# A routed MoE kernel: ReLU's output transposed by VectorE and DRAM in place of TensorE, the second product two slots behind, weight splits placed in branches of each slot

## The chip, the cores and the metric

The kernel runs on one core of a Trainium2 chip. The time is that of one execution on the device, in microseconds (us); lower is better. A core has five engines with instruction streams of their own: TensorE (PE), VectorE (DVE), ScalarE (ACT), GpSimd (POOL) and SyncE (SP). They meet only at semaphores and through transfers (DMA) that an engine issues and the DMA engines carry out.

## The reference

A block-causal attention over 8 batches, 8 heads, 576 positions and a head width of 64 gives 4608 rows (tokens) of 512 numbers. Each row is then sent to one of 8 experts:

```python
logits = x @ w_gate
expert_idx = np.argmax(logits, axis=1)
probs = np.exp(logits - logits.max(-1, keepdims=True))
probs /= probs.sum(-1, keepdims=True) + 1e-09
gate_w = probs[np.arange(N), expert_idx]
for e in range(E):                       # 8 experts
    mask = expert_idx == e
    if not mask.any():
        continue
    xe = x[mask]
    h = np.maximum(xe @ w1[e], 0.0)      # 512 -> 1024
    ye = h @ w2[e]                       # 1024 -> 512
    out[mask] = gate_w[mask, None] * ye
```

Everything is float32. Which expert a row goes to is known only when the attention has been computed. For the inputs that are timed, the experts get 896, 0, 1030, 58, 512, 192, 384 and 1536 rows.

## The kernel before, in words

Two parts follow each other: the attention with the router (until about 377 us), which the change leaves as it is, and the class `Experts`, where all of the change lies.

**Slots.** The rows of an expert are taken in slots of 128; an expert with n rows has n/128 slots, rounded up. Here that is 7, 9, 1, 4, 2, 3 and 12 slots for the seven experts that have rows, one after the other: slots 0-6, 7-15, 16, 17-20, 21-22, 23-25 and 26-37. The first 36 slots exist whatever the data; for 36 and 37 every engine branches (`tail`, L1173). A small table that DVE works out (`slots`, L732 to L748) tells each slot's expert.

**One slot.** A slot t has these steps; `period(t)` writes them into the engines' streams:

- `gather`: POOL fetches the slot's 128 rows from the DRAM copy `xd` by an indirect DMA.
- `rows_in`: PE transposes the rows, four 128x128 pieces into the PSUM tile `px` (L853).
- `rows_act`, `rows_pool`: ACT rounds `px` to `xh` (L863) and copies it to `xf` (L866); POOL takes `xl = xf - xh` (L872). A float32 number is so split into a high and a low part, and a product is made of three: high by high, low by high, high by low.
- `first_pe`: the first product, 48 matmuls 128x128 by 128x512, 24 each into the PSUM tiles `ph` and `o` (L894). Its weights w1 are split in the same way.
- `relu_act`: ACT writes ReLU of `ph` and `o` to `h` (L930), 128 rows by 512 each.
- `hidden_pe`, `hidden_act`, `hidden_low`: PE transposes each half of `h` into `pt` (L938, four matmuls), ACT rounds it to the high part (L948; the trace calls this tile `low`, after the pool that it lies in) and copies it to `hf` (L952), and POOL subtracts (L958).
- `second_pe`: the second product, 24 matmuls into `py` (L978), in two halves of 12.
- `out_act`, `out_pool`: ACT scales `py` by the gate to `y` (L995), POOL scatters it to the output by an indirect DMA (L1001).

**Order.** It is written out by hand. On PE a period is: first product of t, `rows_in` of t+1, transposes of the first half of h of t, half of the second product of t-1, transposes of the second half, the other half of the second product of t-1. So the second product runs one slot behind the first.

**Weights.** An expert's weights are eight chunks of 128x1024: four of w1, four of w2. SP loads them (L1095) into five buffers `raw`; DVE copies each chunk to its high part (L1102) and subtracts for the low part (L1108). There are two halves of the weight buffer `w`, used in turn by the experts. DVE splits the next expert's w1 as soon as the first product of the last slot of the expert before the running one is done, and its w2 as soon as that slot's second product is done (a wait on a count read from the table, L1157). This is a loop over the eight experts ahead of all of the slots: it has no place in the slots' order.

**End.** `finish` does the last slot's second product and the last two slots' outputs.

The PE order, the ACT order and the lines above are the ones that the change touches.

## Time and profile before

| | |
|---|---|
| median of 3 runs | 861.5 us (858.24 to 861.5) |
| the profiled execution, its own time | 861.02 us |
| the profiled execution, its span | 859.2 us |
| mean granted TensorE clock in it | 0.994 |
| attention and router | to about 377.6 us |
| start of the expert part, until the slots run evenly | 377.6 to 405.3 us |
| slots 3 to 37, 35 slots | 405.3 to 840.1 us |
| the last output | 840.1 to 859.2 us |

The span runs from the first instruction of the trace to its last; what is left to the execution's own time, 1.8 us, lies around it. In the rows of a profile, a line such as L938 is a line of the kernel before, an engine's name stands ahead of the operation, and `out<-in` are the tiles that it writes and reads. `PEclk` is the clock that TensorE was granted, 1.00 being full speed.

### The profile page before, as it was taken

The numbers are of one execution on the slowest core, as the hardware profiler recorded it, in microseconds if no ns is written. First come the engines' busy times: TensorE is split into PE (matmuls) and PEld (weight loads), VectorE is DVE, ScalarE is ACT, GpSimd is POOL, SyncE is SP. The second block draws the span as 40 slices with busy tenths as digits, with TensorE's granted clock in tenths as the row PEclk, the third lists the DMA queues.
The fourth block names the chain that finished last, engine by engine and source line by source line (L and its number), as shares of the span: only waits on it lengthen the run. The fifth ranks groups of instructions, "written<-read, shape, count | busy, mean of one in ns | idle before, by whom it ended". The sixth has DMA issues, their size and how long they took to land.

```text
span 859.2 us, 15869 instructions
## 1 busy us (share of the span) xinstructions
PE 828.8 (96%) x4936; PEld 634.4 (74%) x4936; DVE 391.3 (46%) x1144; ACT 457.0 (53%) x1154; POOL 394.9 (46%) x394
## 2 busy tenths in 40 slices
PE   4999999999999999989999999999999999999993
PEld 2666666666666676668888888888888888888882
DVE  3567676767676767668615000058356450000000
ACT  3777677777777777724443443343344434433430
POOL 4121244444444624255746444556566564445451
PEclk9999999999999999999999999999999999999997
DMA  5229726363635355425614311146436431111110
GB/s 174 73 96 188 206 96 164 96 161 111 157 103 139 120 119 179 102 48 194 219 50 138 133 50 50 38 135 209 166 123 245 142 111 38 50 50 37 38 51 28
DMA packets 45687, 99.33 MB, mean 116 GB/s; under 512 B 7585, under 2 KB 10913, under 8 KB 45602
## 3 DMA queue, kind: packets, MB, share of 16 engines
q1 hardware_dynamic: 38082, 78.26, 31.3%
q0 software_dynamic: 7520, 19.97, 6.8%
q8 instruction: 49, 0.80, 0.4%
q14 instruction: 36, 0.29, 0.1%
HBM read 76.76 MB, written 21.98 MB: 115 GB/s over the span
## 4 chain that ended last, share of the span: by engine, by line
PE 91%; DMA 3%; ACT 1%; POOL 1%; issue 1%; SPq 1%; DVE 0%; POOLq 0%; ACTq 0%; DVEq 0%
PE py L978 24%; PE ph L894 12%; PE o L894 12%; PE o L270 11%; PE ya L169 6%; PE xa L169 4%; PE pt L938 4%; PE o L305 3%; PE px L853 2%; DMA xd<-xg 2%; ACT pb L200 1%; PE o L299 1%; DMA qd<-qT 1%; PE o L158 1%; DMA out<-y,idx 1%
## 5 line engine op out<-in xcount | busy, mean ns | idle before, releaser
L978 PE MATMUL py<-w,low 128*128 (+1 forms) x912 | 231.5, 403 | 0.1
L978 PEld LDWEIGHTS py<-w,low 128*128 128x128 f32 x912 | 166.4, 189 | 35.4 <-issue 0.5
L112 POOL TENSOR_SCALAR q<-qd 128x640 f32<-128x640 f32 x32 | 58.0, 1812 | 189.4 <-PE o L158 124.3
L1102 DVE CAST w<-raw 128x1024 fp32r<-128x1024 f32 x60 | 52.9, 931 | 185.6 <-PE o L894 135.1
L958 POOL TENSOR_TENSOR low<-hf,low 128x512 fp32r<-128x512 f32 x72 | 98.9, 1374 | 35.6 <-ACT hf L952 35.6
L872 POOL TENSOR_TENSOR xl<-xf,xh 128x512 fp32r<-128x512 f32 x38 | 51.4, 1354 | 90.8 <-ACT xf L866 90.6
L1108 DVE TENSOR_TENSOR w<-raw,w 128x1024 fp32r<-128x1024 f32 x60 | 82.6, 1434 | 0.0
L948 ACT CAST low<-pt 128x512 fp32r<-128x512 f32 x76 | 45.7, 601 | 58.2 <-PE pt L938 56.9
L200 ACT ACTIVATE pb<-ya,neg 128x320 f32<-128x320 f32 (+2 forms) x96 | 50.1, 525 | 48.1 <-DVE neg L185 48.1
L894 PE MATMUL o<-w,xh 128*128 x280 | 75.6, 392 | 0.0
L894 PE MATMUL ph<-w,xh 128*128 x280 | 75.6, 392 | 0.0
L1001 POOL DMA_INDIRECT out<-y,idx x35 | 40.0, 1144 | 65.9 <-ACT y L995 65.9
L169 PE MATMUL ya<-kd,q 64*128 64x192 f32 (+2 forms) x192 | 61.8, 456 | 2.7 <-ACT pb L200 2.7
L930 ACT ACTIVATE h<-o 128x512 f32<-128x512 f32 x37 | 22.2, 599 | 74.7 <-PE o L894 74.7
L169 PE MATMUL yb<-kd,q 64*128 64x192 f32 (+2 forms) x192 | 61.8, 457 | 0.0
L995 ACT ACTIVATE y<-py,xg 128x512 f32<-128x512 f32 x38 | 26.2, 690 | 66.3 <-PE py L978 60.8
L894 PEld LDWEIGHTS ph<-w,xh 128*128 128x128 f32 x280 | 52.6, 188 | 11.6
L894 PEld LDWEIGHTS o<-w,xh 128*128 128x128 f32 x280 | 52.6, 188 | 11.5
L930 ACT ACTIVATE h<-ph 128x512 f32<-128x512 f32 x37 | 22.2, 599 | 73.1 <-PE ph L894 73.1
L689 POOL DMA_INDIRECT tab<-toks,posi x40 | 41.8, 1044 | 27.3 <-DVE run L656 13.8
L200 ACT ACTIVATE pb<-yb,neg 128x192 f32<-128x192 f32 (+2 forms) x96 | 49.8, 526 | 0.4 <-DVE neg L185 0.4
L952 ACT COPY hf<-pt 128x512 f32<-128x512 f32 x76 | 46.3, 609 | 6.0 <-POOL low L958 5.2
(953 smaller groups left out, 1805.3 us busy)
## 6 DMA issues: line engine op xcount, KB each, us to landing
raw<-w SPq DMA_DIRECT2D x60, 512.0 KB, 5.5
qd<-qT SPq DMA_DIRECT2D x32, 352.0 KB, 3.4
v<-vt SPq DMA_DIRECT2D x32, 352.0 KB, 4.6
kd<-kT SPq DMA_DIRECT2D x32, 288.0 KB, 4.0
xd<-xt SPq DMA_DIRECT2D x7, 1026.0 KB, 8.5
xd<-xg SPq DMA_DIRECT2D x9, 256.5 KB, 12.1
xg<-w SPq DMA_DIRECT2D x8, 256.0 KB, 3.9
xd<-x SPq DMA_DIRECT2D x8, 128.0 KB, 3.8
```

The costliest lines, as they stand in the source:

```text
L112: self.nc.gpsimd.tensor_scalar(q, self.raws[m][0][:, 0 : 512 + P], 0.125, None, ALU.mult)
L169: ins = mm(out, q[r, 128 * (i - 1) : 128 * i], k[r, o : o + n], start=True, stop=True, skip_group_check=True)
L200: ins = self.nc.scalar.activation(dst, src, AF.Exp, bias=self.neg[m][:, c : c + 1], scale=1.0, accum_out=self.sums[m][:, c : c + 1])
L270: self.nc.tensor.matmul(out[r], self.raws[m][2][:, slot], self.ph[m, bank][:, c0:c1], start=t in (0, 5), stop=t in (4, 5), skip_group_chec ...
L872: pool.tensor_sub(self.xl, self.xf, self.xh).then_inc(sem["xp"], 1)
L894: m = pe.matmul(self.ph[f], x[:, P * k : P * k + P], weights(k, f, part), start=start and k == 0, stop=stop and k == 3,)
L948: act.copy(self.hh[t % 2][:, f], self.pt[f]).then_inc(sem["ha"], 1)
L952: act.copy(self.hf, self.pt[f]).then_inc(sem["ha"], 1)
L958: engine.tensor_sub(self.hl[t % 2][:, f], self.hf, self.hh[t % 2][:, f]).then_inc(sem["hp"], 1)
L978: m = pe.matmul(self.py[t % 2], h[:, c // 4, P * (c % 4) : P * (c % 4) + P], wf[:, bass.ds(off + (base + 512 * c), 512)], start=n == 0, st ...
L1102: dve.tensor_copy(hi, raw[m % nr]).then_inc(sem["wh"], 1)
L1108: dve.tensor_sub(lo, raw[m % nr], hi).then_inc(sem["wd"], 1)
```

## The change

**The transposes of h.** After the change PE does not transpose h from slot 3 on, and ACT and POOL do not read it out of PSUM. `blocks(t, f)`: DVE transposes each half of h in blocks of 32x32 into `hblk`, laid out so that a block stands where it is needed within its 32 partitions. `leave(t)`: ACT issues one DMA of `hblk` (128x1024, 512 KB) to a DRAM buffer `there`. `enter(t)`, a slot later: ACT issues four DMAs of 128 KB back from DRAM, each for 32 partitions, which brings the blocks into the right partitions. `split_act`: one ACT copy of 128x1024 makes the high part; `split_pool`: two POOL subtractions of 128x512 the low part. They stand in place of four ACT instructions and two of POOL.

**The lag.** The second product of a slot runs two slots behind its first product: period t has `second_pe(t - 2)`. At the transition, period 3 still has the second product of slot 2, period 4 has none, and period 5 has that of slot 3. The output is three slots behind. Five buffers `xg` instead of four hold the gathered rows, and ACT issues DMAs, which it did not do in the slots before.

**The weight splits.** The loop over the experts is gone. Eight chunks are four units of two chunks (two copies, two subtractions). DVE's stream has, in each period t after `blocks(t)`, the w2 units of period t-1 and the w1 units of period t; which of them are done is read from a table `pk` in each slot and decided by branches. `pieces`, 18 small DVE operations with one copy more in `slots`, makes that table. The plan it gives: the next expert's units 0 to 3 go one to each of the running expert's first slots, and where it has fewer than four slots, several to the first: an expert with three slots has units 0 and 1 in its first slot, with two slots 0 to 2, with one slot all four. For slots 0 and 1 the plan counts as if the first expert began at slot 2. The raw buffers are four instead of five, and SP loads only the experts that have rows (48 loads in place of 56 in that loop).

On PE, between the last matmul of the first product and the first of the second, the stream of one slot reads before:

```order
L894 MATMUL o<-w,xh 128x512
L853 MATMUL px<-ident,xg_192 128x128 x4
L938 MATMUL pt_4960<-ident,h_4955 128x128 x4
L966 REGISTER_ALU
L978 ISA
L978 MATMUL py_4962<-w,low_75 128x512
```

and after:

```order
L940 MATMUL o<-w,xh 128x512
L899 MATMUL px<-ident,xg_193 128x128 x4
L1066 UNCONDITIONAL_BRANCH
L1066 REGISTER_ALU
L1083 ISA
L1083 MATMUL py_4969<-w,low_77 128x512
```

The four transposes of h (`pt`) are gone, the same holds for the four in the middle of the second product, and a jump has come in that closes the block of DVE's branches.

ACT's stream of one slot, with the semaphores that an instruction waits for in brackets, reads before (y is scaled, h is ReLU's output, `low` the high part of the transposed h, `hf` its copy):

```order
L995 ACTIVATE y<-py_4962,xg_192 128x512 [waits y,mm2]
L930 ACTIVATE h_4955<-ph_4958 128x512 [waits ht,mm1]
L930 ACTIVATE h_4956<-o 128x512 [waits ht,mm1]
L863 CAST xh<-px 128x512 [waits mm1,xt]
L866 COPY xf<-px 128x512 [waits xp]
L948 CAST low_75<-pt_4960 128x512 [waits mm2,ht]
L952 COPY hf<-pt_4960 128x512 [waits hp]
L948 CAST low_75<-pt_4961 128x512 [waits mm2,ht]
L952 COPY hf<-pt_4961 128x512 [waits hp]
```

and after:

```order
L1100 ACTIVATE y<-py_4969,xg_192 128x512 [waits y,mm2]
L1033 DMA high<-there_59 32x4x256 [waits ln,hn,dw]
L1033 DMA high<-there_59 32x4x256 x3
L978 ACTIVATE h_4962<-ph_4965 128x512 [waits tb,mm1]
L978 ACTIVATE h_4963<-o 128x512 [waits tb,mm1]
L909 CAST xh<-px 128x512 [waits mm1,xt]
L912 COPY xf<-px 128x512 [waits xp]
L1022 DMA there_60<-hblk 128x1024 [waits tb]
L1044 CAST low_77<-high 128x1024 [waits mm2,dr]
L1066 UNCONDITIONAL_BRANCH
```

Two transfers of a slot now stand in ACT's stream with waits in front: the read of slot t-1 ahead of ReLU of slot t, waiting for the write of slot t-1 (`dw`); and the rounding of slot t-1 behind it, waiting for that read (`dr`).

DVE's stream before has nothing of the slots, only the splits. The start of one expert's w1, with the read of the count (`si`) of the slots ahead of the running expert, is:

```order
L1157 TENSOR_LOAD si
L1157 ISA x2
L1160 ISA
L1102 CAST w<-raw_81 128x1024 [waits raw2,mm1]
L1102 CAST w<-raw_82 128x1024 [waits raw3]
L1102 CAST w<-raw_83 128x1024 [waits raw4]
L1102 CAST w<-raw_79 128x1024 [waits raw0]
L1108 TENSOR_TENSOR w<-raw_81,w 128x1024 [waits wh]
```

After, each slot has the block transposes and then two calls of `units`; these are the rows up to the waits of the first copy of the first call:

```order
L1015 STREAM_TRANSPOSE hblk<-h_4962 128x4x4x32 [waits dw,ra]
L1015 STREAM_TRANSPOSE hblk<-h_4963 128x4x4x32 [waits dw,ra]
L1214 TENSOR_LOAD pk
L1214 ISA x2
L1221 REGISTER_ALU x3
L1221 COMPARE_AND_BRANCH
L1223 COMPARE_AND_BRANCH
L1224 COMPARE_AND_BRANCH
L1226 REGISTER_ALU x3
L1228 ISA [waits mm2]
L1229 REGISTER_ALU [waits raw0]
L1229 REGISTER_ALU x2
```

The copies of four chunks, which stood behind one wait for the buffer's last reader (`mm1`), now stand two by two behind three branches, and behind the block transposes of their slot.

The core of the diff:

```diff
+        def blocks(t, f):
+            dve.wait_ge(sem["ra"], 2 * t + f - 1)
+            if t > EARLY:
+                dve.wait_ge(sem["dw"], 16 * (t - EARLY))
+            else:
+                dve.wait_ge(sem["hp"], 2 * EARLY)
+            dve.transpose(
+                self.ht.rearrange("p (b f c i) -> p f c b i", b=4, f=2, c=4)[:, f],
+                self.h[f].rearrange("p (c b j) -> p c b j", c=4, b=4),
+            ).then_inc(sem["tb"], 1)
+        def leave(t):
+            act.wait_ge(sem["tb"], 2 * (t - EARLY) + 2)
+            act.dma_start(self.there[t % 2], self.ht).then_inc(sem["dw"], 16)
+        def enter(t):
+            act.wait_ge(sem["dw"], 16 * (t - EARLY + 1))
...
+            view = self.there[t % 2].rearrange("(a j) (b r) -> b j a r", a=4, b=4)
+            for b in range(4):
+                act.dma_start(
+                    self.hp[t % 2][32 * b : 32 * b + 32].rearrange("j (a r) -> j a r", a=4), view[b]
+                ).then_inc(sem["dr"], 16)
+        def split_act(t):
+            act.wait_ge(sem["dr"], 64 * (t - EARLY + 1))
+            act.wait_ge(sem["mm2"], t)
+            act.copy(
+                self.hh[t % 2].rearrange("p f (c a i) -> p (f c) a i", c=4, a=4),
+                self.hp[t % 2].rearrange("p (a g i) -> p g a i", a=4, g=8),
+            ).then_inc(sem["hn"], 1)
+        def split_pool(t):
...
+            for f in range(2):
+                pool.tensor_sub(
...
+                ).then_inc(sem["ln"], 1)
         def period(t):
...
+            first_pe(t)
+            if t != EARLY + 2:
+                out_act(lagging(t))
+                out_pool(lagging(t))
             if t + 2 < NS:
                 gather(t + 2)
+            if t > EARLY:
+                enter(t - 1)
+            for f in range(2):
+                relu_act(t, f)
+                blocks(t, f)
             if more:
+                rows_in(t + 1)
+                rows_act(t + 1)
+                rows_pool(t + 1)
+            leave(t)
+            if t > EARLY:
+                split_act(t - 1)
+                split_pool(t - 1)
+            units(t - 1, 1)
+            units(t, 0)
+            if t != EARLY + 1:
+                for f in range(2):
+                    second_pe(t - 2 + (t == EARLY), f)
         def finish(t):
-            second_pe(t, 0)
-            second_pe(t, 1)
+            enter(t)
+            out_act(t - 2)
+            out_pool(t - 2)
+            split_act(t)
+            split_pool(t)
+            for i in (t - 1, t):
+                second_pe(i, 0)
+                second_pe(i, 1)
...
+        def units(t, second):
+            pk = dve.value_load(self.pk[t : t + 1, 0:1], min_val=0, max_val=8 * 4096 - 1)
+            hi, lo, first, e8 = pk & 7, (pk >> 3) & 7, (pk >> 6) & 63, (pk >> 12) << 3
+            off = 16384 - (((pk >> 12) & 1) << 14)
...
+            with dve.If(hi > lo):
+                for i in (2 * second, 2 * second + 1):
+                    with dve.If(hi > i):
+                        with dve.If(lo < i + 1):
+                            if second:
+                                dve.wait_ge(sem["mm2"], first + 1)
+                            for c in (2 * i, 2 * i + 1):
+                                dve.wait_ge(sraw[c % 4], e8 * 4 + (16 + 16 * (c // 4)))
+                                dve.tensor_copy(part(c, 0), raw[c % 4]).then_inc(sem["wh"], 1)
+                            for c in (2 * i, 2 * i + 1):
+                                dve.wait_ge(sem["wh"], e8 + (9 + c))
+                                dve.tensor_sub(part(c, 1), raw[c % 4], part(c, 0)).then_inc(sem["wd"], 1)
+            dve.end_ifs()
-            for e in range(1, E):
-                row = sp.value_load(self.row[e : e + 1, 0:1], min_val=0, max_val=DM * (E - 1))
-                for c in range(8):
-                    m = 8 * e + c - 4
-                    if m >= nr:
-                        sp.wait_ge(sem["wd"], m)
-                    load(m, row)
...
+            def loads(e):
+                with sp.If(count > e):
+                    row = sp.value_load(self.row[e : e + 1, 0:1], min_val=0, max_val=DM * (E - 1))
+                    for c in range(8):
+                        m = 8 * e + c - 4
+                        sp.wait_ge(sem["wd"], m + 1)
+                        load(m, row)
...
-    raw = [rcst.tile([P, 1024], F32, tag=f"raw{i}", name=f"raw{i}") for i in range(5)]
+    raw = [rcst.tile([P, 1024], F32, tag=f"raw{i}", name=f"raw{i}") for i in range(4)]
```

`mm1` and `mm2` count finished halves of first products and finished second products, `ra` ReLU's outputs, `tb` block transposes, `dw` and `dr` the write to and the read from DRAM, `wh` and `wd` chunks of weights whose high and low part is done, `hn` and `ln` the high and low parts of h.

More of the change, by code (lines that the diff above doesn't have):

```diff
@@ L453 @@
 LATE = 2
+XG = 5
 class Router:
@@ L503, in __init__ @@
         self.first = cp.tile([P, EARLY], I32, tag="first", name="first")
-        self.xg = [cp.tile([P, RW], F32, tag=f"xg{i}", name=f"xg{i}") for i in range(4)]
+        self.xg = [cp.tile([P, RW], F32, tag=f"xg{i}", name=f"xg{i}") for i in range(XG)]
         nc.gpsimd.memset(self.xg[0], 0.0)
@@ L523, in __init__ @@
                 ("off", [P, 1], I32), ("col", [P, 1], I32), ("row", [P, 1], I32),
+            )
+        }
+        self.plan = {
+            k: tp.tile(shape, dt, tag=k, name=k)
+            for k, shape, dt in (
+                ("ranks", [P, 1], F32), ("start", [P, E], F32), ("q", [P, 8], F32), ("count", [P, 1], I32),
+                ("pk", [P, 1], I32),
             )
@@ L748, in slots, with pieces, __init__ @@
         do(v.tensor_scalar(row, n[:, 1:2], float(E - 1), float(DM), ALU.min, ALU.mult))
+        do(v.tensor_copy(self.plan["count"], a[:, 1, E - 1 : E]))
+    def pieces(self, do, bank):
+        v = self.nc.vector
+        each = self.meta["each"]
+        ranks, start, q, count, pk = self.plan.values()
+        a = bank[:, 0 : 2 * E].rearrange("p (a e) -> p a e", a=2)
+        s = bank[:, 4 * E : 4 * E + 3]
+        c = [q[:, i : i + 1] for i in range(8)]
+        do(v.tensor_copy(ranks, a[:, 1, E - 1 : E]))
+        do(v.tensor_sub(start, a[:, 0], each[:, 0]))
+        do(v.tensor_scalar(start, start, self.part, None, ALU.is_le))
+        do(v.tensor_mul(start, start, each[:, 0]))
+        do(v.tensor_reduce(c[0], start, AX.X, ALU.add))
+        do(v.tensor_scalar(c[0], self.part, c[0], 4.0, ALU.subtract, ALU.add))
+        do(v.tensor_copy(c[1], s[:, 0:1]))
+        do(v.tensor_scalar(c[2], self.part, -2.0, c[1], ALU.add, ALU.min))
+        do(v.tensor_max(c[3], c[0], c[2]))
+        do(v.tensor_scalar(c[4], s[:, 2:3], ranks, -1.0, ALU.subtract, ALU.is_lt))
+        do(v.tensor_scalar(c[5], c[2], 0.0, c[4], ALU.is_gt, ALU.mult))
+        do(v.tensor_scalar(c[5], c[3], 4.0, c[5], ALU.min, ALU.mult))
+        do(v.tensor_scalar(c[6], c[3], 1.0, 4.0, ALU.add, ALU.min))
+        do(v.tensor_mul(c[6], c[6], c[4]))
+        do(v.scalar_tensor_tensor(c[7], s[:, 2:3], 64.0, self.part, ALU.mult, ALU.add))
+        do(v.tensor_sub(c[7], c[7], c[1]))
+        do(v.scalar_tensor_tensor(c[7], c[7], 8.0, c[5], ALU.mult, ALU.add))
+        do(v.scalar_tensor_tensor(pk, c[7], 8.0, c[6], ALU.mult, ALU.add))
 class Experts:
-    def __init__(self, ctx, tc, ident, w1, w2, out, router, high, low, y, raw, ph):
+    def __init__(self, ctx, tc, ident, w1, w2, out, router, high, low, y, raw, ph, there):
         self.tc, self.nc, self.router = tc, tc.nc, router
@@ L778, in __init__ @@
         self.xf, self.xh, self.xl = t("xf", [P, 512]), t("xh", [P, 512], F32R), t("xl", [P, 512], F32R)
-        self.h, self.hf = [t("h0", [P, 512]), t("h1", [P, 512])], t("hf", [P, 512])
+        self.h, self.ht = [t("h0", [P, 512]), t("h1", [P, 512])], t("hblk", [P, 1024])
+        self.hf = self.ht[:, 0:512]
+        self.hp = [high.bitcast(F32)[:, 1024 * i : 1024 * i + 1024] for i in range(2)]
+        self.there = there
         self.y = y
@@ L815, in run @@
         sraw = [tc.alloc_semaphore(f"raw{i}") for i in range(nr)]
-        sg = [tc.alloc_semaphore(f"g{i}") for i in range(4)]
+        sg = [tc.alloc_semaphore(f"g{i}") for i in range(XG)]
         sy = tc.alloc_semaphore("y")
@@ L842, in gathered @@
         def gathered(t):
[L844 removed]
+            return len([k for k in range(EARLY, t + 1) if k % XG == t % XG])
         def rows_in(t):
             if t >= EARLY:
[L849 removed]
+                pe.wait_ge(sg[t % XG], 16 * gathered(t))
             if t >= 2:
@@ L1134, in run @@
             dve.sem_inc(sem["me"], 1)
+            self.router.pieces(do, self.bank)
             for f in range(2):
@@ L1148, in run @@
             sp.wait_ge(sem["mm1"], 2 * EARLY + 1)
-            for e in range(1, E):
-                row = sp.value_load(self.row[e : e + 1, 0:1], min_val=0, max_val=DM * (E - 1))
-                for c in range(8):
-                    m = 8 * e + c - 4
-                    if m >= nr:
-                        sp.wait_ge(sem["wd"], m)
-                    load(m, row)
-                if e >= 2:
-                    before = dve.value_load(self.before[e - 1 : e, 0:1], min_val=0, max_val=NS)
-                for half, name, of in ((0, "mm1", lambda: before * 2 + 1), (4, "mm2", lambda: before + 1)):
-                    if e >= 2:
-                        dve.wait_ge(sem[name], of())
-                    for part in (high, low):
-                        for c in range(half, half + 4):
-                            part(8 * e + c - 4)
+            count = sp.value_load(self.count[0:1, 0:1], min_val=1, max_val=E)
+            def loads(e):
[5 more added lines that the diff above has]
+                        load(m, row)
+                    if e + 1 < E:
+                        loads(e + 1)
+            loads(1)
+            sp.end_ifs()
             total = None
@@ L1192, in attention_moe_kernel @@
     tab = dram.tile([P * TC, 1], I32, tag="tab", name="tab")
+    there = [dram.tile([P, 1024], F32, tag=f"there{i}", name=f"there{i}") for i in range(2)]
     rcst = ctx.enter_context(tc.tile_pool(name="rcst", bufs=1))
@@ L1287, in attention_moe_kernel @@
     with ExitStack() as mctx:
-        Experts(mctx, tc, ident, w1, w2, out, router, high, low, y, raw, first[0]).run()
+        Experts(mctx, tc, ident, w1, w2, out, router, high, low, y, raw, first[0], there).run()
 def kernel(**inputs):
```

92 lines of the change are left out of this document (53 added, 39 removed).

## The prediction

> **What bounds the kernel now.** First the page: how busy each engine is, and the shares of the chain of work that ended last.
>
> ```profile
> PE 828.8 (96%) x4936; PEld 634.4 (74%) x4936; DVE 391.3 (46%) x1144; ACT 457.0 (53%) x1154; POOL 394.9 (46%) x394
> PE 91%; DMA 3%; ACT 1%; POOL 1%; issue 1%; SPq 1%; DVE 0%; POOLq 0%; ACTq 0%; DVEq 0%
> ```
>
> TensorE works 96% of the span and carries 91% of the chain. These are averages over two parts, so the busy times by stage come next, for the start of the expert part and for slots 3 to 37.
>
> ```profile
> core 0: us, PE busy (x) PEld busy (x) DVE busy (x) ACT busy (x) POOL busy (x), PEclk, DMA share, GB/s
> 377.58:405.32 27.74, 27.25 (x133) 21.95 (x134) 24.06 (x41) 12.26 (x23) 16.63 (x14) 1.00 0.42 140
> 405.32:840.06 434.74, 434.73 (x2100) 358.47 (x2099) 120.47 (x107) 172.98 (x316) 238.43 (x212) 1.00 0.31 104
> ```
>
> In the 35 slots PE is busy for all of the 434.7 us, at full clock: 12.42 us a slot. DVE has 120 us of work there, ACT 173, POOL 238. So whatever leaves PE is gained in full, and whatever keeps PE waiting is lost in full. The chain through one slot (start, duration, what):
>
> ```profile
> 417.75 2.75 PE ph L894 x12
> 420.50 2.75 PE o L894 x12
> 423.25 0.44 PE px L853 x4
> 423.68 0.44 PE pt L938 x4
> 424.12 2.82 PE py L978 x12
> 426.93 0.44 PE pt L938 x4
> 427.37 2.81 PE py L978 x12
> 430.18 0.92 PE ph L894 x4
> ```
>
> Piece follows piece without a gap. The first product takes 5.5 us, the second 5.63, the rows 0.44, the transposes of h 0.44 twice.
>
> **What goes.** Both `pt` pieces go in slots 3 to 37: 430.18 - 417.75 = 12.42 becomes 11.55 us, and 35 times 0.87 is **-30.5 us**. This is the only gain on the path. The ACT and POOL work that goes is off it. Five further terms say where PE may now wait.
>
> **The start.** DVE makes the table with 19 more small operations, ahead of its subtraction for slot 0:
>
> ```profile
> 387.37 0.15 DVE L747 TENSOR_SCALAR e<-si 128x1 int32<-128x1 int32 x1
> 387.56 0.16 DVE L748 TENSOR_SCALAR row<-n 128x1 int32<-128x1 f32 x1
> 389.31 0.69 DVE L958 TENSOR_TENSOR low<-hf,low 128x512 fp32r<-128x512 f32 x1 [1.59 <-ACT hf L952]
> ```
>
> Such operations come 0.19 to 0.21 us apart, so 19 are some 3.9 us; 1.59 us of them fall into the wait in the last row, and the subtraction moves back by about 2.4. Behind it ACT's next `hf` and DVE's next subtraction move likewise; the second product, which reads them, has part of that in hand. I take **+1.2**, between 0 (all hidden) and 2.4 (none).
>
> **Slot 5.** Period 4 has no second product, so slot 5's first product follows its row transposes directly. The start of the expert part shows such a place:
>
> ```profile
> 384.85 0.45 PE px L853 x4
> ...
> 385.33 0.59 ACT xh L863
> ...
> 385.96 1.20 PE ph L894 x4
> ```
>
> From the end of `px` (385.30) to the product 0.66 us pass; the second ReLU of slot 4 stands ahead of `xh` on ACT and adds some 0.3. These rows price ACT's and POOL's work, and what the transpose may cost:
>
> ```profile
> L930 ACT ACTIVATE h<-ph 128x512 f32<-128x512 f32 x37 | 22.2, 599 | 73.1 <-PE ph L894 73.1
> L952 ACT COPY hf<-pt 128x512 f32<-128x512 f32 x76 | 46.3, 609 | 6.0 <-POOL low L958 5.2
> L872 POOL TENSOR_TENSOR xl<-xf,xh 128x512 fp32r<-128x512 f32 x38 | 51.4, 1354 | 90.8 <-ACT xf L866 90.6
> L958 POOL TENSOR_TENSOR low<-hf,low 128x512 fp32r<-128x512 f32 x72 | 98.9, 1374 | 35.6 <-ACT hf L952 35.6
> L958 DVE TENSOR_TENSOR low<-hf,low x4: 684/688/693, 389.3 to 396.4; 128x512 fp32r<-128x512 f32 x4
> ```
>
> `xl` comes 0.6 + 1.35 us after `xh`, and four matmuls (0.92) cover part: 1.0 more. Together **+2.0**; the period left out of the second products returns at the end, one for one.
>
> **The weight splits.** No block transpose is in the trace. I take 0.7 us for 128x512, the row of DVE's 128x512 subtraction; twice that is the upper bound, zero the lower. Four copies and four subtractions of 128x1024, in two places:
>
> ```profile
> 559.92 3.60 DVE L1102 CAST w<-raw 128x1024 fp32r<-128x1024 f32 x4 [85.42 <-PE o L894]
> 563.44 6.81 DVE L1108 TENSOR_TENSOR w<-raw,w 128x1024 fp32r<-128x1024 f32 x4
> 579.25 2.50 DVE L1102 CAST w<-raw 128x1024 fp32r<-128x1024 f32 x4 [9.00 <-PE py L978]
> 581.67 4.63 DVE L1108 TENSOR_TENSOR w<-raw,w 128x1024 fp32r<-128x1024 f32 x4
> ```
>
> So a unit of two chunks costs 3.6 us at best and 5.2 at worst. The first row shows, too, that before the split of slot 17's w1 started where slot 15's first product ended. Now the expert of slot 16 has one slot, and that split stands behind the transposes of slot 16. With T the end of slot 16's first product: ReLU and transpose 1.5, reading the table and branching about 1, so it starts at T + 2.5 and ends at T + 9.6 to 12.9. Slot 17's product starts at T + 6.1 and reads the low parts 1.84 later (eight matmuls), at T + 7.9. PE waits 1.7 to 5.0; POOL is as busy there as in the rows at 559.92, so **+4.9**.
>
> The experts with four, two and three slots cost less. Three units stand in one period in periods 17, 21 and 23: 10.7 to 15.6 us ahead of the next slot's transposes. In period 17 two of them also wait for the second product that ends with the period, so the transposes of slot 18 end at 12.1 to 17.0 us of their period rather than at 7.1, 5 to 10 late; in the others they are 1.5 to 6.5 late. Late transposes hold `leave`, and behind it on ACT `enter`, the next ReLU and the next rows' rounding: PE feels it when they are late by more than about 5.8: with the write priced below, `enter` can usually start 7.1 + 0.4 + 5.5 - 11.55 = 1.4 us into the next period; it takes 2.0, two ReLUs and `xh` 1.8, and `xl` wants 0.5 more before the period's end at 11.55. That is 0 to 4.2 in period 18 and 0 to 0.7 in the other two; three third units may wait some 0.5 each for their loads: 0 to 7 in all. I take **+4.5**, above the middle, since POOL keeps DVE near its slow rows.
>
> **The way through DRAM.** A write of 512 KB, then four reads of 128 KB. Transfers of these sizes, and issues (the first column after the count is least/median/longest in ns):
>
> ```profile
> raw<-w SPq DMA_DIRECT2D x60, 512.0 KB, 5.5
> xd<-xt SPq DMA_DIRECT2D x7, 1026.0 KB, 8.5
> xd<-x SPq DMA_DIRECT2D x8, 128.0 KB, 3.8
> first<-tab SPq DMA_DIRECT2D x1, 1.5 KB, 2.4
> out<-y,idx POOLq DMA_INDIRECT x35, 2.8
> L1095 SPq DMA_DIRECT2D raw<-w  x56: 332/372/384, 393.0 to 693.5; - x56
> L534 SPq DMA_DIRECT2D xd<-x x8: 593/602/1177, 88.7 to 368.4; - x8
> ```
>
> I take 5.5 us for the write (W), as for the read of that size, between the 2.8 of a scatter of 256 KB and the 8.5 of a write twice as large; 2.6 for a read of 128 KB, between 2.4 and 2.8, with 3.8 as upper bound; 0.5 for an issue on ACT, between 0.37 and 0.6. ACT's loop is then: `leave` 0.4, W, four issues 2.0, two ReLUs 1.2, two row copies 1.2: W + 4.8 = 10.3 us, within the 11.55 of PE. **No cost while W is below 6.75.** The rounding and y fit beside W. POOL's subtractions are as many as before.
>
> [...]
>
> **The last slot.** Nothing follows it but second products. From the end of its first product: ReLU 0.8, transpose 0.7, `leave` 0.4 + 5.5, three issues 1.5, the fourth's landing 2.6, rounding 1.07 (609 ns, plus 512 columns at some 0.9), semaphores 0.2: 12.8 us, against 11.25 of the second products of slots 35 and 36. That is 1.5 of waiting, and POOL's two subtractions (2.75) end 0.9 after the eight matmuls (1.87) that do without them: **+2.4**, between 0 (W 2.8) and 7.
>
> **Sum.** -30.5 + 1.2 + 2.0 + 4.9 + 4.5 + 2.4 = -15.5 on the profiled execution's 861.02 (span 859.2 and 1.8 around it): 845.5. The median of the runs is 0.5 above that execution: **846**.
>
> **The rivals.** *A, slower: ACT's loop is bound by the write.* From W = 6.75 each us more costs 34 us over 34 slots, and above 7.2 the kernel is slower than before. At 7.6 it is 12.4 - 11.55 = 0.85 a slot, 29 us: about 875. For it: a write twice as large took 8.5, the raw loads run at the same time, and every slot carries 1 MB more. Against it: DMA is 0.31 busy in these slots, and the 512 KB reads took 5.5 in them.
>
> *B, nothing waits but the start and slot 5:* the splits run at their fast rows and the write is nearer 2.8. Then 861.0 - 30.5 + 3.2 + 0.5, and 1 for slot 17: about 835. Against it: slot 17 waits 1.7 even with fast rows.
>
> *C, the branches cost.* DVE calls `units` twice a slot.
>
> ```profile
> L1157 DVEq TENSOR_LOAD <-si x6: 304/307/550, 416.9 to 668.7; - x6
> L1157 DVEq FUSED_REGOPS  x6: 190/190/206, 417.4 to 669.4; - x6
> L1173 PEldq COMPARE_BRANCH  x4: 80/1852/3944, 811.7 to 842.2; - x4
> L1173 ACTq COMPARE_BRANCH  x4: 38/42/50, 813.0 to 846.3; - x4
> ```
>
> A branch took 0.04 us on ACT; on PE it took up to 3.9. If a call cost 3.6 us beside the 0.6 of reading the table, DVE would need 7.2 + 1.2 + 1.4 (transposes) + 3.0 (24 units of 4.4 over 35 slots) + 1.3 (other instructions) = 14.1 us a slot, more than 11.55: 35 x 2.55 = 89, about 920, and the shorter PE slot would then bring nothing at all. It decides from some 2.3 us a call. I count 0.05 to 0.1 a branch, ACT's row: the skipped code of a unit is short. [...]
>
> **How the numbers follow.** Forecast 0.63, with a range of its own of 838 to 857 from the terms' ends; A 0.16; B 0.14; C 0.07. About 0.5% is what a measurement here can tell from no change. Of A some 0.06 stays within that bound (W 7.1 to 7.4) and 0.10 lies above it, with C's 0.07. Of the forecast 0.01 reaches it. So faster 0.76, same 0.07, slower 0.17. The range runs from 834 to 868: B's end below, and above it A up to W = 7.4, which leaves 0.2 out.
>
> **What would show it.** Right: no L938-like transposes from slot 3 on, slots of 11.55 us, PE gaps at slots 5, 17, 18 to 25 and at the end only, `leave` landing in 5 to 6 us, block transposes of about 0.7 us. ACT waiting for `there` in most slots, with periods above 11.55, is A; long DVE branches are C. Wrong most easily: W, the price of a block transpose, and how DVE's splits and POOL's subtractions slow each other.

## The result, and the profile after

| | before | changed |
|---|---|---|
| median, in the runs made together | 861.5 us (858.24 to 863.1) | 847.35 us (846.09 to 848.88) |
| ratio of the times, 95% interval | | 0.9841 (0.9808 to 0.9874) |
| the profiled execution, its own time | 861.02 us | 846.09 us |
| its span | 859.2 us | 844.3 us |

The change makes the kernel 1.6% faster; 846 was forecast. The page of the changed kernel, its busy times and the shares of the chain that ended last (its lines are those of the changed kernel: L940 is the first product, L1083 the second):

```profile
PE 802.0 (95%) x4656; PEld 604.5 (72%) x4656; DVE 434.2 (51%) x1217; ACT 419.4 (50%) x1049; POOL 395.5 (47%) x394
PE 83%; issue 4%; DVE 4%; DMA 3%; POOL 2%; ACT 2%; DVEq 1%; ACTq 0%; POOLq 0%; SPq 0%
```

TensorE's share of the chain has gone from 91% to 83%: it is still the bound, but now and then it waits. The busy times of the stage that was full before, and of one short stretch in it, of which more below:

```profile
core 0: us, PE busy (x) PEld busy (x) DVE busy (x) ACT busy (x) POOL busy (x), PEclk, DMA share, GB/s
405.32:840.00 434.68, 415.52 (x1851) 335.08 (x1850) 161.94 (x163) 137.11 (x213) 244.41 (x218) 0.99 0.56 183
570.80:575.20 4.40, 4.40 (x12) 3.50 (x13) 2.12 (x2) 0.00 (x0) 0.12 (x1) 0.61 0.94 355
```

In the first of these windows DVE has 41 us more than before, ACT 36 less; the DMA engines are busy for 0.56 of the time in place of 0.31. One quiet slot in the chain:

```profile
439.63 2.75 PE ph L940 x12
442.38 2.75 PE o L940 x12
445.12 0.44 PE px L899 x4
445.56 5.60 PE py L1083 x24
451.16 2.75 PE ph L940 x12
```

The slot is 451.16 - 439.63 = 11.53 us, the `pt` pieces are gone, and nothing waits. Where TensorE does wait is read from its timeline; these are the groups with a gap ahead of them, from slot 3 on (in brackets the gap and what ended it), and the group ahead of the first:

```profile
406.78 1.07 PE L940 MATMUL ph<-w,xh 128*128 x4
409.30 1.20 PE L940 MATMUL ph<-w,xl 128*128 x4 [1.44 <-POOL xl L918]
427.16 1.18 PE L940 MATMUL ph<-w,xh 128*128 x4 [1.01 <-ACT xh L909]
428.74 1.19 PE L940 MATMUL ph<-w,xl 128*128 x4 [0.39 <-POOL xl L918]
570.80 1.51 PE L940 MATMUL ph<-w,xh 128*128 x4 [4.17 <-DVE w L1229]
603.99 4.00 PE L1083 MATMUL py<-w,low 128*128 x16 [0.45 <-POOL low L1054]
674.02 4.00 PE L1083 MATMUL py<-w,low 128*128 x16 [0.33 <-POOL low L1054]
678.95 1.20 PE L940 MATMUL ph<-w,xh 128*128 x4 [0.93 <-ACT xh L909]
680.49 1.20 PE L940 MATMUL ph<-w,xl 128*128 x4 [0.33 <-POOL xl L918]
819.27 11.50 PE L1083 MATMUL py<-w,low 128*128 x48 [0.86 <-issue]
```

They lie in slots 3, 5, 17, 20, 26 and at the end. A gap is less than what it costs, since the matmuls beside it are slower: in these rows four of them took 1.18 to 1.51 us right behind a gap, 1.07 in the group ahead of the first. So the costs are taken from the distances between the row transposes (`px`, L899): what slot t costs is the distance from its `px` to that of slot t+1, less the 11.55 us of a quiet slot.

| place | from | us |
|---|---|---|
| transposes of h | 35 x 0.87 | -30.5 |
| start | `px` of slot 3 at 403.10, before at 401.48 | +1.6 |
| slot 3 | 10.90, before 9.17 | +1.7 |
| slot 5 | 7.88, without a second product (5.60) | +1.9 |
| slot 17 | 17.56 | +6.0 |
| slot 20 | 12.38 | +0.8 |
| slot 26 | 14.06 | +2.5 |
| end, from the last `px` (812.21, before 832.95) | the moved second product and the transposes taken out | +1.1 |
| sum | | -14.9 |

Measured are -14.9 between the two profiled executions.

### The profile page after: what moved, and what is told of

Its sections match the earlier page's. It is cut to its first block, busy times and chain, and to the rows that moved or that the text cites. A ratio compares the mean times of both kernels' runs of the same rounds, so it can differ in the third digit from the quotient of the medians.

```text
span 844.3 us, 16283 instructions
## 1 busy us (share of the span) xinstructions
PE 802.0 (95%) x4656; PEld 604.5 (72%) x4656; DVE 434.2 (51%) x1217; ACT 419.4 (50%) x1049; POOL 395.5 (47%) x394
## 4 chain that ended last, share of the span: by engine, by line
PE 83%; issue 4%; DVE 4%; DMA 3%; POOL 2%; ACT 2%; DVEq 1%; ACTq 0%; POOLq 0%; SPq 0%
PE py L1083 21%; PE o L270 12%; PE ph L940 10%; PE o L940 10%; PE ya L169 7%; PE xa L169 4%; PE o L305 4%; PE px L899 1%; DMA raw<-w 1%; DMA there<-hblk 1%; PE o L299 1%; ACT pb L200 1%; PE o L158 1%; DVE w L1232 1%; POOL xl L918 0%
## 5 line engine op out<-in xcount | busy, mean ns | idle before, releaser
L1083 PE MATMUL py<-w,low 128*128 (+1 forms) x912 | 223.0, 399 | 1.7 <-issue 0.9
L1083 PEld LDWEIGHTS py<-w,low 128*128 128x128 f32 x912 | 168.1, 188 | 41.3 <-POOL low L1054 1.9
L1015 DVE STREAM_TRANSPOSE hblk<-h 128x512 f32<-128x512 f32 x70 | 48.9, 706 | 216.0 <-ACT h L978 135.3
L1054 POOL TENSOR_TENSOR low<-high,low 128x512 fp32r<-128x512 f32 x70 | 101.8, 1474 | 32.1 <-ACT low L1044 32.1
L940 PE MATMUL ph<-w,xh 128*128 x280 | 77.0, 397 | 6.1 <-DVE w L1229 4.2
L940 PE MATMUL o<-w,xh 128*128 x280 | 75.5, 391 | 0.0
L1232 DVE TENSOR_TENSOR w<-raw,w 128x1024 f32 x48 | 70.1, 1499 | 0.0
L1106 POOL DMA_INDIRECT out<-y,idx x35 | 42.7, 1221 | 52.9 <-ACT y L1100 42.8
L940 PEld LDWEIGHTS ph<-w,xh 128*128 128x128 f32 x280 | 53.0, 190 | 19.2 <-issue 7.2
L1229 DVE CAST w<-raw 128x1024 f32 x48 | 49.1, 1060 | 30.5 <-issue 22.2
L940 PEld LDWEIGHTS o<-w,xh 128*128 128x128 f32 x280 | 52.6, 188 | 11.4
L1044 ACT CAST low<-high 128x1024 fp32r<-128x1024 f32 x35 | 36.7, 1050 | 44.8 <-DVE hblk L1015 21.2
```

Of the source, the lines that this page charges most:

```text
L940: m = pe.matmul(self.ph[f], x[:, P * k : P * k + P], weights(k, f, part), start=start and k == 0, stop=stop and k == 3,)
L1015: dve.transpose(self.ht.rearrange("p (b f c i) -> p f c b i", b=4, f=2, c=4)[:, f], self.h[f].rearrange("p (c b j) -> p c b j", c=4, b=4), ...
L1054: pool.tensor_sub(self.hl[t % 2][:, f].rearrange("p (c a i) -> p c a i", c=4, a=4), inner(t)[:, f], self.hh[t % 2][:, f].rearrange("p (c a ...
L1083: m = pe.matmul(self.py[t % 2], h[:, c // 4, P * (c % 4) : P * (c % 4) + P], wf[:, bass.ds(off + (base + 512 * c), 512)], start=n == 0, st ...
L1229: dve.tensor_copy(part(c, 0), raw[c % 4]).then_inc(sem["wh"], 1)
L1232: dve.tensor_sub(part(c, 1), raw[c % 4], part(c, 0)).then_inc(sem["wd"], 1)
```

## Experiments

The last two columns are what slot 17, and slots 18 to 26 together, take above 11.55 us each. The time is that of the profiled execution; where no median stands beside it, the kernel was run once.

| kernel | time, us | slot 17 | slots 18 to 26 |
|---|---|---|---|
| changed, first profile | 846.09 | 6.0 | 3.3 |
| changed again | 848.88 (median 850.65) | 5.9 | 3.7 |
| e2, two writes | 855.12 | 7.3 | 8.6 |
| e3, four writes | 889.63 | 11.5 | 26.2 |
| e4, lag of one | 878.37 | 4.7 | 29.4 |
| e5, start | 846.82 (median 846.18) | 6.9 | 4.8 |
| e6, early units | 860.61 (median 860.61) | 0.0 | 23.7 |
| e7, e5 and e6 | 859.11 (median 859.38) | 0.0 | 23.6 |
| e8, early in a single slot | 845.61 (median 845.81) | 0.0 | 10.1 |
| e9, e5 and e8 | 843.10 (median 842.93) | 0.0 | 9.5 |
| e10, no loads | 844.15 | 6.8 | 0.0 |
| e11, e8 without loads | 839.59 | 0.0 | 0.0 |

### TensorE's transposes put back

```diff
+        def idle_pe(f):
+            for k in range(4):
+                pe.transpose(self.pt[f][:, P * k : P * k + P], self.ident, self.ident)
...
+                idle_pe(0)
...
+                    if f == 0:
+                        idle_pe(1)
```

> The changed kernel, with eight 128x128 transposes put back on TensorE in each slot from 3 on, at the two places where they stood before; they transpose a constant into a PSUM tile that nobody reads and wait for nothing. Forecast's theory (TensorE's own instructions set the slot): the slot goes from 11.55 back to 12.42 us; 35 x 0.87 = 30.5 us, less at most two or three slots in which TensorE waits anyway: 874 to 877 us, that is slower than the kernel before, since the waits that the change brought stay. Rival (part of the gain came from ScalarE, GpSimd, the transfers or the fewer weight loads, and TensorE's transposes were only a cover for them): the slot stays below 12.2 us and the time below 868.

Measured: 877.79 us, a little above the range expected, and the kernel before took 862.75 on that chip. The row transposes of two neighbouring slots in TensorE's timeline:

```profile
744.23 0.60 PE L899 MATMUL px<-ident,xg 128*128 128x128 f32 x4
756.65 0.60 PE L899 MATMUL px<-ident,xg 128*128 128x128 f32 x4
```

12.42 us again. The whole gain is TensorE's instructions: with them back, the kernel is some 15 us slower than before, which is the price of the change's waits. The rival falls.

### The write made longer

```diff
         def leave(t):
             act.wait_ge(sem["tb"], 2 * (t - EARLY) + 2)
+            for i in range(3):
+                act.dma_start(self.spare[i], self.ht).then_inc(sem["dw"], 16)
             act.dma_start(self.there[t % 2], self.ht).then_inc(sem["dw"], 16)
```

This is the kernel with four writes; with two, the loop runs once. The waits for the write count all of the writes.

> The changed kernel, with h written to DRAM twice in each slot on ScalarE's queue (512 KB to a buffer that nobody reads, then the real one; the wait is for both). Loop theory: W is the time from the first write's issue to the second's landing; ScalarE's loop is 0.34 a write + W + four read issues 1.8 + four row instructions of 0.6, that is W + 4.5 with one write (W 3.1) and W + 4.9 with two. It binds above 11.55 us, from W = 6.7. With W of 4.3 to 5.5 the slot stays 11.55 us; the time grows by at most 5 us, in the slots in which the splits hold DVE and at the end: 846 to 851 us. Rival (transfers and not the loop are the limit: each byte more costs, since the DMA engines are shared with the weight loads): every slot grows, by over 0.3 us, 857 us or more.

> The same with four writes of 512 KB in each slot, the last the real one. Loop theory: ScalarE's loop is 1.4 + W + 4.2 us; with W of 6.5 to 9 it is 12.1 to 14.6 us and binds: the slot's length follows it one for one, 0.5 to 3 us above 11.55, 865 to 950 us in all, and slot length minus the measured W is 5.6 within 0.5. Rival (a long round trip is hidden by the lag of two slots whatever its length): the slot stays 11.55 us, below 855. A slot that grows by much more than the loop gives would speak for the DMA engines' bandwidth as the limit.

Two writes: 855.12 us, between the two expectations. No slot outside 17 to 26 grew, so the rival that every byte costs falls; but slots 17 to 26 lose 15.9 us in place of 9.3, more than I expected, and another 1.9 are lost behind the last `px`. Four writes: 889.63 us. In slots 27 to 37 the slot stays 11.55 us even so. Where it grows, ACT's timeline shows the loop, from one write's issue to the next:

```profile
449.19 1.77 ACTq L1023 DMA_DIRECT2D there<-hblk  x3
...
461.25 1.78 ACTq L1035 DMA_DIRECT2D high<-there  x4
463.12 0.60 ACT L978 ACTIVATE h<-ph 128x512 f32<-128x512 f32 x1 [8.46 <-issue]
...
465.09 1.65 ACTq L1023 DMA_DIRECT2D there<-hblk  x3
```

Here W runs from the first issue to the start of the reads: 12.06 us; the loop takes 15.90. The rest is 3.84: four read issues 1.87 and four row instructions of some 0.5 each, since ACT's instructions overlap a little (these are 0.59 to 0.62 us long and start 0.46 to 0.53 apart). In another place it is 8.53 and 12.52, 3.99 apart. So the loop is W + 3.9, and it binds from W = 7.6, not 6.75. I had expected 5.6 for the rest, having counted the write issues twice; in slots 27 to 37 W is 7.4 in the median, right at the bound. Slots 6, 7 and 8 took 12.81, 11.55 and 17.92 us beside loops of 12.90, 11.39 and 15.90; slot 8 took 2.0 more than its loop, and its first three groups of four matmuls, behind a wait of 3.27 us, took 1.91 to 2.07 us each, against 1.08 or 1.09 in the slot before. Rival A's mechanism is shown. With one write, the change stays clear of the bound by 4.5 us where the write takes its median of 3.1, and by 0.6 at the longest write, 7.0.

### A lag of one slot

```diff
-            return t - 3 + (t < EARLY + 2)
+            return t - 2
...
-            if t != EARLY + 1:
-                for f in range(2):
-                    second_pe(t - 2 + (t == EARLY), f)
+            for f in range(2):
+                second_pe(t - 1, f)
```

ACT issues the reads first in the slot, and rounds between the two ReLUs; this reordering was not tried without the lag.

> The changed kernel, with the second product one slot behind the first, as before the change, in place of two; ScalarE's and GpSimd's order in the slot is turned so that the read is issued first and the split stands between the two ReLUs. Theory with the measured transfers: from the end of the first product ReLU 0.8, transpose 0.7, write 3.4, read 4.0, rounding 1.05 give the high part after 10.1 us, and TensorE wants it after 11.99; the low part after 13, wanted after 13.9: slots stay at 11.55 us where no split is in the way. Gone is the gap of slot 5 (1.9 us), new are 3 to 4 us at the end, and late block transposes have no slack: 1 to 12 us more in slots 17 to 25. In all 847 to 860 us. By the write as forecast (5.5 us) the low part would come 1.5 us late in every slot: about 900. Rival (the lag of two is needed, the chain through DRAM is longer than a slot): each slot grows by over 1 us, 880 or more.

Measured: 878.37 us. Neither expectation holds: the slots without splits, 27 to 37, stay at 11.55 us (`px` at 751.27 and 762.82), but the time is far above 860.

```profile
751.27 0.60 PE L899 MATMUL px<-ident,xg 128*128 128x128 f32 x4
762.82 0.60 PE L899 MATMUL px<-ident,xg 128*128 128x128 f32 x4
...
855.38 7.92 PE L1083 MATMUL py<-w,low 128*128 x24 [5.53 <-ACT low L1044]
```

So the round trip through DRAM fits where no split is in the way, and the second slot of lag isn't needed there. Slots 18 to 26 lose 29.4 us in place of 3.3, slots 7 and 12 0.9 and 1.4 in place of none, and the last second product waits 5.5. The lag of two is a store of time for the slots with splits and loads; I had allowed 1 to 12 us for them.

### The start

```diff
             self.router.slots(cnt, do, self.bank)
             dve.sem_inc(sem["me"], 1)
-            self.router.pieces(do, self.bank)
...
                 dve.tensor_copy(self.w[:, 0, 0, o], self.high[:, o]).then_inc(sem["wh"], 2)
+            self.router.pieces(do, self.bank)
...
-        do(v.tensor_scalar(c[2], self.part, -2.0, c[1], ALU.add, ALU.min))
+        do(v.tensor_scalar(c[2], self.part, -3.0, c[1], ALU.add, ALU.min))
```

> The changed kernel as it is, for comparison on the same chip: 846 to 849 us; slot 3 waits about 1.5 us for xl, slot 5 1.9, slot 17 6.0, slots 20 and 26 together 3.3.

> The changed kernel, with the 18 table operations behind the copies of the first expert's w1 instead of ahead of slot 0's subtraction, and with the first expert's units counted from slot 3 instead of slot 2, so that VectorE splits nothing in period 2. Theory: the table delays the second product of slot 0 (1.35 us), and VectorE's two copies and two subtractions in period 2 hold up GpSimd's first output scatter (4.87 us against 1.48 before the change), so xl of slot 3 comes late (1.6 us with the slow matmuls behind it). Both go: 2.5 to 3.0 us less than the changed kernel in the profiled run, the scatter at 1 to 2 us, first product of slot 3 without a gap. Rival (the scatter is long for its own reasons, as a first of its kind): it stays above 4 us and only 1.3 us go.

GpSimd's timeline has the first output scatter; first the changed kernel, with the copy of the next slot's indices behind it:

```profile
401.59 4.87 POOL L1106 DMA_INDIRECT out<-y,first  x1 [8.57 <-ACT y L1100]
406.44 0.23 POOL L877 COPY idx<-stab 128x1 int32 x1
```

In the same stretch DVE copied and subtracted, up to 405.57:

```profile
399.75 2.36 DVE L1296 CAST w<-high 128x2048 fp32r<-128x2048 f32 x2
402.02 1.29 DVE L1229 CAST w<-raw 128x1024 f32 x2
403.22 2.35 DVE L1232 TENSOR_TENSOR w<-raw,w 128x1024 f32 x2
```

And in the kernel with the other start:

```profile
401.65 1.01 POOL L1106 DMA_INDIRECT out<-y,first  x1 [6.55 <-ACT y L1100]
402.63 0.23 POOL L877 COPY idx<-stab 128x1 int32 x1
```

1.01 us instead of 4.87, with no split beside it, and slot 3 lost its gap: from `px` of slot 3 to that of slot 4 it is 9.18 us in place of 10.89. The rival (a scatter that is slow by itself) falls. Up to slot 3 the other start brings 1.6 us more: from `px` of slot 2 to that of slot 3 it is 16.73 us, 18.30 in the changed kernel. In slots 17 to 26 e5 lost 2.0 us of what it had gained. The medians, 846.18 and 850.65, differ by more than what is left, 1.3 us. Runs also differ ahead of slot 2 (its `px` came at 384.77 and 387.34 us in the two profiles of the changed kernel, at 386.42 in e5's); what the rest of the medians' difference is, isn't shown.

### Splits ahead of the transposes

```diff
+        def early_units(t):
+            pk = dve.value_load(self.pk[t - 1 : t, 0:1], min_val=0, max_val=8 * 4096 - 1)
+            late = ((pk >> 6) & 63) + ((((pk & 7) + 1) >> 2) << 6)
+            with dve.If(late < 63 + t):
+                units(t - 1, 1)
+                units(t, 0)
...
+            late = early_units(t)
             for f in range(2):
                 relu_act(t, f)
                 blocks(t, f)
...
-            units(t - 1, 1)
-            units(t, 0)
+            with dve.If(late > 62 + t):
+                units(t - 1, 1)
+                units(t, 0)
```

A unit of w1 then waits for the last first product that reads its half of the buffer.

> The changed kernel, with the w1 units of period t (and the w2 units of t-1 ahead of them) put ahead of the block transposes of slot t, so that the split starts when the last reader of the buffer is done, except in the two periods in which the w2 units have to wait for that period's own second product; those stay behind the transposes (a second set of branches). Theory: slot 17's wait is the split standing behind slot 16's transposes and the reading of the table; the split then starts some 9 us earlier, and the wait of 6.0 us goes down to at most 1; slots 20 and 26, now 3.3 us together, to 0 to 3, since the transposes come at most as late as now. 5 to 8 us less than the changed kernel: 838 to 842 us. Rival (units ahead of the transposes delay them, and the round trip behind them, by as much as is gained): slots 17, 22 or 24 lose 3 us or more each, and the time stays within 2 us of the changed kernel.

> Both edits together, the start and the early units. Theory: the gains lie in different slots and add: 8 to 11 us less than the changed kernel, 835 to 839 us. If the first expert's units, one slot later, meet the next expert's start, it is less than the sum by more than 1 us.

860.61 and 859.38 us: the rival's mechanism holds, in other slots than it named and at a higher price, for the two kernels are 10 and 9 us slower than the changed one (850.65). Slot 17's wait is gone altogether, but in e6 slots 20, 23 and 25 lose 10.0, 5.7 and 8.2. Ahead of slot 17, e6 loses 0.8 in slot 8, e7 0.3 in slot 6 and 2.3 in slot 9. DVE's timeline in e6 ahead of slot 23's loss:

```profile
631.28 0.68 DVE L1243 CAST w<-raw 128x1024 f32 x1
636.02 0.69 DVE L1243 CAST w<-raw 128x1024 f32 x1 [4.06 <-DMA raw<-w]
636.63 2.35 DVE L1246 TENSOR_TENSOR w<-raw,w 128x1024 f32 x2
638.90 1.30 DVE L1015 STREAM_TRANSPOSE hblk<-h 128x512 f32<-128x512 f32 x2
```

A copy waits 4.06 us for its load, and the transposes stand behind it. Ahead of the transposes, a wait for a load is in the way of the write of h and of all that hangs on it.

### Early only where the next slot needs it

```diff
-            pk = dve.value_load(self.pk[t - 1 : t, 0:1], min_val=0, max_val=8 * 4096 - 1)
-            late = ((pk >> 6) & 63) + ((((pk & 7) + 1) >> 2) << 6)
-            with dve.If(late < 63 + t):
+            pk = dve.value_load(self.pk[t : t + 1, 0:1], min_val=0, max_val=8 * 4096 - 1)
+            late = ((pk & 63) + 60) & 63
+            with dve.If(late < 1):
```

This is shown against e6's kernel; behind the transposes the condition is now `late > 0`. `late` is 0 only where a slot does the units 0 to 3, all of a split.

> As e6_early, but the units go ahead of the transposes only in the first slot of an expert with one slot (here slot 16, whose four units are the next expert's whole split); everywhere else they stand behind them as in the changed kernel. Theory after e6_early: early units help where the next slot needs them at once and hurt where a wait for a raw load then stands ahead of the transposes. Slot 17's wait of 6.0 us goes, slot 16's transposes end within their room; the later slots (3.3 us together in the changed kernel) stay within 2 us of that. 4 to 6 us less than the changed kernel: 841 to 845 us. Rival (e6_early's loss comes from the second set of branches and their table reads, not from the place of the units): the second set is still there in every slot, so slots 20 to 26 lose over 8 us together and the time is 850 or more.

> e8_single with the start of e5_start. Theory: the two gains lie in different slots; about 3 us less than e8_single at the start, 7 to 9 us less than the changed kernel: 838 to 843 us, ratio to the kernel before 0.971 to 0.977. If the gain at the start is given back in the slots with splits, as e5_start gave back some 1.5 of its 3 us, 841 to 845.

845.81 us (ratio to before 0.9831, 0.9806 to 0.9857) and 842.93 us (0.9793, 0.9772 to 0.9813). e8's time lies a little above the range expected, and its theory was wrong: slot 17's 6 us went, and slots 18 to 26 lost 10.1 in place of 3.3. The gain was given back. e9's time lies in the range expected, its ratio above the 0.971 to 0.977, and the gains did not add: its slots 17 to 26 lose 9.5 us, as much as in the changed kernel (9.3 and 9.6), so it has only the gain of the start. It is the fastest of the kernels with loads, though e5 with 0.979 (0.9752 to 0.9829) can't be told from it.

### The loads left out

```diff
-                                dve.wait_ge(sraw[c % 4], e8 * 4 + (16 + 16 * (c // 4)))
...
-            loads(1)
-            sp.end_ifs()
```

> The changed kernel without the 48 loads of the later experts' weights (SyncE's loop) and without VectorE's waits for them: every split reads the chunks that lie in the raw buffers from the first expert, so the output of the later experts is not the reference's. All splits and branches stay. Theory: slot 17's wait is the place of the split and not a load, so its 5 to 7 us stay; of the 3.3 us in slots 20 and 26 at most 1 stays, since without the loads the write lands after 2.8 us in every slot and no third unit waits: 841 to 845 us. Rival (VectorE's copies, subtractions and table reads alone hold the transposes too long): slots 20 and 26 keep over 2 us together.

> e8_single without the loads, in the same way. There slot 17's wait was gone and slots 20 to 26 lost 10 us together. Theory: what was given back there is the load traffic, which slot 17's wait had given time (raw loads and the write and read of h share the DMA engines): without loads slots 17 to 26 lose at most 2 us together, 835 to 839 us. Rival (the limit is VectorE's order: three units in one period ahead of the next transposes, whatever the loads do): they keep 4 us or more, 840 to 845.

In both the slots came out as the theory had it; e10's time, 844.15 us, lies in its range, e11's, 839.59, 0.6 above. Without loads, slots 18 to 26 are all at 11.55 us in both kernels, and slot 17 keeps its wait where the split is late. TensorE there, without loads, in the order of the change and with e8's (a gap, and none):

```profile
561.52 5.84 PE L1083 MATMUL py<-w,low 128*128 x24
571.52 2.07 PE L940 MATMUL ph<-w,xh 128*128 x4 [4.17 <-DVE w L1228]
```

```profile
563.25 5.85 PE L1083 MATMUL py<-w,low 128*128 x24
568.94 1.09 PE L940 MATMUL ph<-w,xh 128*128 x4
```

So two causes are shown: slot 17 is the place of the split, slots 18 to 26 are the loads, and what e8 gave back is the loads too. e11 has the second set of branches as well and loses nothing, so e8's rival falls. How the loads hurt is in the timelines. In e10 VectorE's order alone still makes transposes late:

```profile
597.86 1.29 DVE L1015 STREAM_TRANSPOSE hblk<-h 128x512 f32<-128x512 f32 x2
```

These are slot 18's. They end 8.1 us behind the end of its first product (`px` of slot 19 at 591.04), 6.6 later than in a quiet slot (1.5), and cost nothing; slot 24's end 7.2 late. In the changed kernel the same are 7.7 and 8.7 late, and the chain that ended last goes there through a load of weights and, ahead of slot 26's wait, a write of h:

```profile
588.58 5.90 DMA raw<-w
...
669.87 5.27 DMA there<-hblk
```

In e10 the write takes 2.9 us in the median. So the loads do both: with them, copies wait and the transposes come another 1.1 and 1.5 us later, and at slot 26 the write beside them takes 2.4 us longer. How the 3.3 us divide between the two isn't shown.

## Why the prediction was right, point by point

**TensorE bounds, and 0.87 a slot is gained in full:** right, -30.5; e1 shows it from the other side.

**The start, +1.2:** the first second product came 1.3 later (394.13 against 392.79), slot 3's `px` 1.6. But a wait was missing: slot 3's `xl`, +1.7. I had put the first expert's split in period 2 at nothing and had not asked whom it holds. e5 shows that it holds GpSimd's scatter, and the subtraction for `xl` stands behind that.

**Slot 5, +2.0:** 1.9, with the two waits named (`xh` 1.01, `xl` 0.39 and the slower matmuls).

**Slot 17, +4.9:** 6.0, above the 1.7 to 5.0 forecast, at the place given and with the split late as described. DVE's timeline of slot 16, from its second transpose:

```profile
561.26 0.71 DVE L1015 STREAM_TRANSPOSE hblk<-h 128x512 f32<-128x512 f32 x1 [2.04 <-ACT h L978]
564.56 2.55 DVE L1229 CAST w<-raw 128x1024 f32 x2 [2.58 <-issue]
567.03 2.41 DVE L1232 TENSOR_TENSOR w<-raw,w 128x1024 f32 x2
569.37 1.28 DVE L1229 CAST w<-raw 128x1024 f32 x2
570.58 2.35 DVE L1232 TENSOR_TENSOR w<-raw,w 128x1024 f32 x2
```

With T = 560.6, the end of slot 16's product, the split starts at T + 4.0 and not T + 2.5: the reads of the table with their branches, of two calls, take 2.6 us where I had about 1. It ends at T + 12.3, inside the 9.6 to 12.9 forecast. TensorE waits for something else than I said: not the low parts but the high parts of the third and fourth chunk (569.37, ended 570.65), which stand behind the first unit's subtractions. That is 4.2 us. The other 1.85 were not in the sum: after the wait the twelve matmuls took 4.61 us in place of 2.75, and the window from 570.80 shows a granted clock of 0.61.

**Slots 18 to 26, +4.5:** 3.3, in slots 20 and 26. Three units in one period, late transposes, a late `leave` and a late `enter` are there, but the sizes were not: I gave the most to period 17's units (0 to 4.2) and at most 0.7 to each of the other two; slot 20 behind period 17 lost 0.8, slot 26 behind period 23 lost 2.5. And I gave the loads some 0.5 each, while without them (e10) nothing is lost. That 4.5 came near 3.3 is in part luck.

**The end, +2.4, and the write, 5.5:** this was the mis-sized step. On the page, the group of the block transposes and the DMA line of the write (35 writes, 70 transposes):

```profile
L1015 DVE STREAM_TRANSPOSE hblk<-h 128x512 f32<-128x512 f32 x70 | 48.9, 706 | 216.0 <-ACT h L978 135.3
there<-hblk ACTq DMA_DIRECT2D x35, 512.0 KB, 3.1
```

The waits on the same tile, `there`, give the spread:

```profile
DMA to landing us min/median/max: 2.6/3.1/7.0
```

The write lands after 3.1 us in the median, not 5.5, and after up to 7.0 where weights are loaded: from 560 to 700 us it took 4.0 in the median; from 700 us on, where no load runs, 2.8 and at most 3.4. At the end the last second product waits for nothing; what is lost is 0.86 ahead of slot 36's second product (818.41 to 819.27) and 0.35 behind the last matmul. For the 0.86 the profile names no engine, but it has a long branch of TensorE's own there:

```profile
L1324 PEldq COMPARE_BRANCH  x4: 77/2076/4836, 791.3 to 827.8; - x4
```

The longest of the four starts at 814.1, during slot 35's second product, and ends at 818.9, 0.3 ahead of slot 36's; so it is likely what TensorE waits for, but this was not tried. The transpose was priced at 0.7 us: 0.706.

**Rival A:** its mechanism is real (e3), its point is W = 7.6 and not 6.75, and the write stays below. **Rival B** had the write right (2.8) and lost on slot 17 (6.0 in place of 1), slot 3 and the slots with loads. **Rival C:** the branches of DVE took 0.05 us (least, median and longest, in ns; the two other lines of branches in `units` at most 80):

```profile
L1223 DVEq COMPARE_BRANCH  x72: 43/52/72, 398.9 to 687.3; - x72
L1214 DVEq TENSOR_LOAD <-pk x71: 301/315/1057, 397.6 to 814.4; - x71
```

The reading of the table, 0.3 us and more, costs more than its branches. That a branch is cheap because the skipped code is short was an estimate; no run shows it.

**The signs:** `leave` landing in 5 to 6 us did not come, and there are gaps in slots 3 and 26, which the list had not.

TensorE as the bound and its 30.5 us are shown; that the sum was right to 0.6 us is luck, because errors cancelled: the start, slot 3 and slot 17 came 3.2 us dearer, slots 18 to 26 and the end 2.5 cheaper. With the measured 3.1 us in place of 5.5 the prediction's own working gives no wait at the end and 0 to 3.3 us in place of 0 to 7 for slots 18 to 26, an estimate of 839 to 842 us; the better price would have made the forecast worse.

## What to carry to other kernels

Here one engine was busy without a gap (434.73 of 434.74 us in slots 3 to 37), and what left it was gained one for one: 0.87 us a slot, and with it back (e1) the slot was at 12.42 us again. The price of the longer way around it was paid at the start, in slots 3, 5, 17, 20 and 26 and at the end; the other slots took 11.55 us. So look for the slots in which other work stands ahead of it in a queue. A wait removed there may come back a few slots on, if transfers set the pace behind it, as slot 17's 6.0 us did in e8 (10.1 us lost in slots 18 to 26 in place of 3.3); leaving the transfers out in an experiment tells the two apart (nothing lost in e11). And a lag that looks like plain latency can be the store from which the bad slots live: with a lag of one (e4) slots 18 to 26 lost 29.4 us in place of 3.3.

## What the hardware showed that was not expected

A wait of 4.17 us cost TensorE another 1.85 us: the granted clock was 0.61 in the 4.4 us behind it, while it was 1.00 in the stretch from 427.0 to 431.0, behind a wait of 1.01. In e4, behind the wait of 5.53 us, the 24 matmuls of the last second product took 7.92 us, those of the one before it 5.84. From how long a wait on the clock falls, and when it comes back, no run shows.

DVE's copies and subtractions held a scatter that GpSimd was issuing for 4.87 us, against 1.01 without them; it ended 0.9 us after the last subtraction (406.46 and 405.57). The scatter waits for one semaphore only, ScalarE's `ya` (`out_pool`, L1105): what DVE did reached it without a semaphore between the two. By what means DVE holds it no run shows, nor how much of the 4.87 us the copies hold and how much the subtractions.
